# A gated mix of linear attention and a GLU: where the denominators of two token groups are summed, and where the T sums of p stand

## The chip, the cores and the metric

The kernel runs on one core of a Trainium2 chip. The metric is the device time of one execution in microseconds (us), lower is better. Before the change the median of three runs is 732.84 us (732.48 to 736.08).

## The reference

For 2048 tokens of width 640, two blocks read the same x and are mixed by a gate per token:

```python
def _A_ref(x, wqkv, wo):                 # linear attention, H = 32 heads, Dh = 20
    q, k, v = ...                        # (x @ wqkv), split by head
    phi = lambda t: jnp.where(t > 0, t + 1, jnp.exp(t)) + 1e-6
    pq, pk = phi(q), phi(k)
    kv = jnp.einsum("bhsd,bhse->bhde", pk, v)
    z = jnp.einsum("bhsd->bhd", pk)
    num = jnp.einsum("bhqd,bhde->bhqe", pq, kv)
    den = jnp.einsum("bhqd,bhd->bhq", pq, z)[..., None] + 1e-6
    return (num / den) ... @ wo
def _B_ref(x, w_gate, w_up, w_down):     # F = 1536
    return (_sigmoid(x @ w_gate) * (x @ w_up)) @ w_down
g = _sigmoid((x * gate_w).sum(-1, keepdims=True))
return g * a + (1 - g) * b
```

The change concerns den, the denominator of each token and head: the sum over 20 features of phi(q) times z.

## The kernel before, in words

All is computed transposed: features on the 128 partitions, tokens along the row. The tokens lie in four groups g of TG = 512. Products are made as three fp32r matmuls each (high and low halves, `mm3`, lines 407 to 409), and most products of 2x2 blocks with seven in place of eight products (the steps s1 to s7 of `Block`, line 1324, and `down_pair`, line 1976), whose sums are made by DVE.

The program has these stages: k and its statistics (to about 145 us); q for groups 2 and 3, with kv (`q_phase(1)`); the GLU for groups 2 and 3 (`f_phase(1)`, twelve blocks f of 128 features of F); q for groups 0 and 1 (`q_phase(0)`, about 407 to 446 us of the profile); the GLU for groups 0 and 1 (`f_phase(0)`, to about 665 us); and the product of scaled phi(q) with the folded kv and wo, with the final mix. The call with `pr = 0` is the second pass over the weights: there the forms of the weights made in the first pass are loaded again from DRAM. Each block f needs three tiles: wg, wu and ws (`load_form`, line 1236), issued on SP after the steps s2, s6 and s7 that read the old ones (line 2274). Each odd f from 3 on also runs `down_pair` for the two blocks ahead of it, with a tile wf in three transfers (`load_wf`, line 1668), issued after s7.

phi(q) without its 1e-6, which is added when it is read, is called p here. `phi_q` (line 1380) makes one tile of p, 128 x 512, for a group g and a feature chunk u (five chunks, KC = 5): ACT makes the exponential and the relu, DVE joins them (line 1388), and a POOL transfer stores the tile to `p_dram`. The feature axis is ordered so that each partition belongs to a head.

The denominators are made by `queue_dens` (line 1432). For each (g, u) a tile of p is read back from `p_dram` into a tile named pden (one of the four buffers of the pool tag "t"), and DVE adds p times `zcol[:, u]` to `fac[:, g]` (five sums per group, line 1442). Then POOL stores the sum to `den_dram`; SP reads it back turned, so that the four parts of a head meet (`turn_in`, four transfers named fac<-den_dram and one of gates, gs); DVE makes gate / den (`factor`: two adds, a reciprocal, a product); POOL stores it to `fac_dram`; and SP reads it back spread over the partitions (`turn_out`, four transfers fac<-fac_dram). `dens` (line 2219) starts groups 2 and 3 at f = 2 and groups 0 and 1 at f = 3 of pr = 0.

`queue_tp` (line 1792) makes the T sums: it reads eight tiles of p of groups 2 and 3 (tile pt), scales them by fac, and stores four sums and differences of each column to `pt_dram`. It is queued at f = 4. `queue_m` (line 1724) reads the folded matrix m (tile mr, four transfers), splits it and stores it to `mp_dram`, five times over, and then makes its sums (`queue_msf`); the first is called after (f, s) = (3, 7), line 2620.

The order on the engines is made by a planner, the class `Order` (line 31), as the program is built. It holds estimated times of PE, ACT and DVE. Work that may wait stands in lists (streams with due times, items, lazy, chain, spare), and `fill` (line 116) takes an item out when its data are expected to be there and it would end within a set slack of PE. `need(key)` runs a list up to that key at once. The engines then run what was written, each in that order; SP and POOL issue their transfers in the order of the program.

Of the kernel before, what the change touches and what calls it, by code (L numbers as in the profile page):

```python
# [374 lines left out]
def gated_mix_kernel(ctx: ExitStack, tc: tile.TileContext, xt, xn, wk, wv, wo, wst_q, wst_f, out_t):  # L375
# [46 lines left out]
    def vec2(out, a, b, op, after=""):  # L422
        order.on_vec(width(out), after, 1.0, out, a, b)
        nc.vector.tensor_tensor(out, a, b, op=op)  # L424

    def vec3(out, a, scalar, b, op0, op1, after=""):
        order.on_vec(width(out), after, 1.0, out, a, b)
        nc.vector.scalar_tensor_tensor(out, a, scalar, b, op0=op0, op1=op1)

    def vec1(out, a, s0, s1=None, op0=OP.mult, op1=None, after=""):  # L430
        order.on_vec(width(out), after, 1.0, out, a)
        if op1 is None:
            nc.vector.tensor_scalar(out, a, s0, None, op0=op0)
        else:
            nc.vector.tensor_scalar(out, a, s0, s1, op0=op0, op1=op1)
# [10 lines left out]
    def add(out, a, b, after=""):  # L446
        vec2(out, a, b, OP.add, after)
# [773 lines left out]
    def tt(name, dt=F32, shape=(P, TG)):  # L1221
        return pw.tile(list(shape), dt, name=name, tag="t", bufs=4)
# [101 lines left out]
    class Block:  # L1324
# [51 lines left out]
        def s7(self):  # L1376
            prod(self.cc, [self.xb(2, 2 + j, 2 + j) for j in range(2)] + [self.xb(2, 4, 4)], False)
            add(self.c12, self.cc, self.c12, "p")

    def phi_q(g, u, src, after="p"):  # L1380

        e = tt("qe")
        act(e, src, AF.Exp, after)
        r = src if after == "v" else tt("qr")
        act(r, src, AF.Relu)

        def rest():
            vec3(e, e, 1.0, r, OP.min, OP.add)
            gp.dma_start(p_dram[:, u, g], e)
        order.need("phi")  # L1390
        order.follow(v_cost(TG), rest, "phi")

# [34 lines left out]
    def gates():  # L1427
        if not gate_sum:
            gate_sum.append(down_pool[1].tile([P, TG], F32, name="gs", tag="far"))
        return gate_sum[0]  # L1430

    def queue_dens(*gs2):

        st = {}

        def load(g, u):
            if u < KC:
                st[g, u] = tt("pden")
                sp.dma_start(st[g, u], p_dram[:, u, g])
                st["at", g, u] = lambda: order.when(st[g, u]) + 1.5  # L1440

        def one(g, u):
            td = fac[:, g]
            if u == 0:
                vec1(td, st[g, u], zcol[:, 0:1], zeps[:, 0:1], OP.mult, OP.add)
            else:
                vec3(td, st[g, u], zcol[:, u:u + 1], td, OP.mult, OP.add)
            load(g, u + 2)
            if u == KC - 1:
                gp.dma_start(den_dram[:, g], td)  # L1450
                st["at", g, u + 1] = lambda: order.when(den_dram[:, g])

        def turn_in(g):
            for j in range(4):
                js = slice(j * H, (j + 1) * H)
                sp.dma_start(fac[js, g].rearrange("h (d c) -> h d c", c=P),
                                  den_dram[:, g, j * P:(j + 1) * P].rearrange("(d h) c -> h d c", h=H))
            st[g, "gs"] = gates()[:, g * P:(g + 1) * P]
            sp.dma_start(st[g, "gs"], gate_rep[4 * g:4 * g + 4].rearrange("i h c -> (i h) c"))
            st["at", g, KC + 1] = lambda: max(order.when(fac[:, g]), order.when(st[g, "gs"])) + 2.5  # L1460

        def factor(g):
            td = fac[:, g]
            q = td[:, :P]
            add(td[:, :2 * P], td[:, :2 * P], td[:, 2 * P:])
            add(q, q, td[:, P:2 * P])
            order.on_vec(5 * P, "")
            nc.vector.reciprocal(q, q)
            vec2(q, q, st[g, "gs"], OP.mult)
            gp.dma_start(fac_dram[:, g], q)  # L1470
            st["at", g, KC + 2] = lambda: order.when(fac_dram[:, g])

        def turn_out(g):
            for d in range(4):
                sp.dma_start(fac[d * H:(d + 1) * H, g].rearrange("h (j c) -> h j c", c=P),
                                  fac_dram[:, g].rearrange("(j h) c -> h j c", h=H))
            FAC_AT[g] = lambda: order.when(fac[:, g]) + 2.5
        order.add(0, 0, lambda: [load(g, u) for u in range(2) for g in gs2], chain=True)
        for u in range(KC):
            for g in gs2:  # L1480
                order.add(0, v_cost(TG), lambda g=g, u=u: one(g, u), None, lambda g=g, u=u: st["at", g, u](), chain=True)
        for n, (v, fn) in enumerate(((0, turn_in), (2.0, factor), (0, turn_out))):
            for g in gs2:
                order.add(0, v, lambda g=g, fn=fn: fn(g), ("fac", g) if n == 2 else None,
                          lambda g=g, n=n: st.get(("at", g, KC + n), lambda: 1e9)(), first=True)

    sp.t = max(sp.t, gp.cell[0])
    load_w()
# [256 lines left out]
    FAC_AT = {}  # L1745

    def queue_msf(i):

# [43 lines left out]
    def queue_tp(j):  # L1792

        src = ((2, j), (2, 2 + j), (3, j), (3, 2 + j))
        raw = []

        def load():
            for g, u in src:
                raw.append(tt("pt"))
                sp.dma_start(raw[-1], p_dram[:, u, g])  # L1800

        def total(n):
            b11, b21, b12, b22 = raw
# [427 lines left out]
    def f_phase(pr, q, hooks={}):  # L2231
# [70 lines left out]
        for f in range(FC):  # L2302
            if f % 2:
                order.need(("h", f // 2 - 1, "B22"), False)
            down = iter(())
            if not pr and f == 4:
                for j in range(2):
                    queue_tp(j)
            if f in dens[pr]:
                queue_dens(*dens[pr][f])  # L2310
            if f % 2 and f > 1:
                if pr:
                    pass
                elif f == FC - 1:
                    for g in range(4):
                        order.need(("fac", g), False)
                    load_m(0)
                down = down_pair(pr, f // 2 - 1)
            for s in (3, 4, 5):
                step(f, s)  # L2320
                next(down, None)
                if s == 3 and f % 2 and f > 1:
                    queue_h(f // 2 - 1, "T4")
                    queue_h(f // 2 - 1, "T3")
                if pr and s == 4:
                    if f < 2 or f % 2:
                        queue_d(("f", 1, f))
                    if f % 2 and f < FC - 1:
                        queue_ds(f // 2)
                    if f == 1:  # L2330
                        queue_df(0)
            if f + 1 < FC:
                step(f + 1, 1)
            else:
                queue_t1(f // 2)
                step(f, 6)
            for _ in down:
                pass
            if f % 2:
                if f < FC - 1:  # L2340
                    queue_t1(f // 2)
                if pr:
                    if f == FC - 1:
                        load_last_s()
                    elif f > 1:
                        queue_df(f // 2)
                    if f < FC - 1:
                        queue_d(("f", 1, f + 1))
            if f + 1 < FC:
# [264 lines left out]
    def a_fifth():  # L2614
# [330 lines left out]
```

## Time and profile before

| | before |
|---|---|
| median of three runs | 732.84 us |
| the profiled execution: its own time | 734.26 us |
| its span in the profile | 732.6 us |
| PE busy | 721.8 us, 99% of the span |
| DVE busy | 588.2 us, 80% |
| ACT busy | 370.0 us, 51% |
| mean rate of the DMA | 263 GB/s |

A row of the timeline gives the start in us from the span's start, the duration, the engine, the line of the kernel, the operation, the tile written and the tiles read (buffer numbers left out), the number of instructions, and in brackets how long the engine was idle before it and what ended that. SPq and POOLq are the queues of transfers that SP and POOL issue: the duration is that of the issue, not of the transfer. Matmuls overlap, so a row's duration is longer than the step from one matmul to the next.

### The profile page before, as it was taken

How to read it: one execution, taken by the hardware profiler on the slowest of the kernel's cores; microseconds unless marked ns; L12 is line 12 of the kernel's file. 1: busy time of each engine (PE TensorE's matmuls, PEld its weight loads, DVE VectorE, ACT ScalarE, POOL GpSimd, SP SyncE). 2: the span in 40 equal slices, each digit the busy share in tenths (PEclk: the TensorE clock that was granted, in tenths of full speed). 3: DMA queues.
4: the chain of work that ended last, by engine and by line, in shares of the span. 5: the costliest groups of instructions: out<-in, count | busy, mean ns of one | idle time of the engine just before them, and what ended most of it. 6: DMA issues, size and time to landing. Idle time of an engine off the chain costs nothing.

```text
span 732.6 us, 10285 instructions
## 1 busy us (share of the span) xinstructions
PE 721.8 (99%) x3545; PEld 617.1 (84%) x3545; DVE 588.2 (80%) x1026; ACT 370.0 (51%) x682; POOL 111.4 (15%) x180
## 2 busy tenths in 40 slices
PE   9999999999999999999999999999799999999998
PEld 8999999988888888888888888888588878787876
DVE  6898878987787889888999954568668789799894
ACT  5884649357667644444455754353324242445450
POOL 0211111113212211211111132000000011011200
PEclk9999999999999999999999999999999999999999
DMA  7577689698787856657687899869979897979946
GB/s 258 157 219 187 179 219 256 146 347 279 273 322 264 317 204 230 232 222 265 247 310 269 243 329 370 339 201 284 355 227 363 253 353 274 374 283 329 193 117 210
DMA packets 83034, 192.30 MB, mean 263 GB/s; under 512 B 12666, under 2 KB 40586, under 8 KB 79270
## 3 DMA queue, kind: packets, MB, share of 16 engines
q1 hardware_dynamic: 62598, 120.41, 49.8%
q0 software_dynamic: 20240, 71.06, 29.1%
q8 instruction: 28, 0.46, 0.3%
q14 instruction: 24, 0.20, 0.1%
q10 hardware_dynamic: 144, 0.16, 0.1%
HBM read 114.12 MB, written 73.56 MB: 256 GB/s over the span
## 4 chain that ended last, share of the span: by engine, by line
PE 85%; DMA 9%; DVE 3%; SPq 1%; ACT 1%; issue 1%; ACTq 0%; DVEq 0%
PE ch L407 9%; PE ch L408 9%; PE ch L409 9%; PE cc L407 8%; PE cc L408 8%; PE cc L409 8%; PE dd L407 6%; PE dd L408 6%; PE dd L409 6%; PE rot L408 5%; PE rot L407 5%; PE rot L409 5%; DMA wu<-wf 2%; DMA wf<-wd 2%; DMA mr<-m_dram 2%; DMA ws<-wf 1%
## 5 line engine op out<-in xcount | busy, mean ns | idle before, releaser
L420 ACT ACTIVATE c<-ch 128x512 f32<-128x512 f32 x54 | 32.2, 597 | 89.1 <-PE ch L409 84.6
L424 DVE TENSOR_TENSOR hf<-c,hf 128x512 fp32r<-128x512 f32 x80 | 54.5, 686 | 22.1 <-ACT hf L420 21.7
L420 ACT ACTIVATE hf<-c 128x512 fp32r<-128x512 f32 x80 | 49.0, 624 | 30.6 <-DVE c L424 30.5
L424 DVE TENSOR_TENSOR c<-cc,c 128x512 f32<-128x512 f32 x42 | 28.9, 689 | 33.8 <-ACT c L420 17.5
L407 PE MATMUL ch<-xth,ws 128*128 128x512 f32 x112 | 43.9, 392 | 2.2 <-DMA ws<-wf 2.2
L409 PE MATMUL ch<-xth,ws 128*128 128x512 f32 x112 | 43.6, 390 | 0.0
L408 PE MATMUL ch<-xtl,ws 128*128 128x512 f32 x112 | 43.6, 389 | 0.0
L424 DVE TENSOR_TENSOR tb<-rot,tb 128x512 f32<-128x512 f32 (+1 forms) x58 | 37.5, 674 | 3.6 <-PE rot L409 3.6
L424 DVE TENSOR_TENSOR c<-c,c 128x512 f32<-128x512 f32 x52 | 35.7, 687 | 1.8 <-ACT c L420 1.1
L407 PE MATMUL dd<-xrh,wg 128*128 128x512 f32 x90 | 35.2, 391 | 0.0
L409 PE MATMUL dd<-xrh,wg 128*128 128x512 f32 x90 | 35.0, 389 | 0.0
L408 PE MATMUL dd<-xrl,wg 128*128 128x512 f32 x90 | 35.0, 389 | 0.0
L420 ACT ACTIVATE c<-dd 128x512 f32<-128x512 f32 x22 | 13.1, 597 | 43.3 <-PE dd L409 43.2
L407 PE MATMUL cc<-xbh,ws 128*128 128x512 f32 x84 | 32.7, 389 | 0.0
L409 PE MATMUL cc<-xbh,ws 128*128 128x512 f32 x84 | 32.7, 389 | 0.0
L408 PE MATMUL cc<-xbl,ws 128*128 128x512 f32 x84 | 32.7, 389 | 0.0
L420 ACT ACTIVATE dd<-ch 128x512 f32<-128x512 f32 x22 | 12.8, 582 | 34.8 <-PE ch L409 34.8
L424 DVE TENSOR_TENSOR tb<-dd,tb 128x512 f32<-128x512 f32 x36 | 24.7, 685 | 5.7 <-PE dd L409 5.7
L407 PEld LDWEIGHTS ch<-xth,ws 128*128 128x128 f32 x112 | 21.0, 188 | 7.1 <-DMA ws<-wf 3.0
L424 DVE TENSOR_TENSOR wst<-wst 128x256 f32<-128x256 f32 (+1 forms) x65 | 24.6, 395 | 1.4
L424 DVE TENSOR_TENSOR tb<-cc,tb 128x512 f32<-128x512 f32 x36 | 24.5, 685 | 1.3 <-PE cc L409 1.3
L409 PEld LDWEIGHTS ch<-xth,ws 128*128 128x128 f32 x112 | 21.0, 188 | 4.7 <-DVE ws L424 0.2
(697 smaller groups left out, 2380.7 us busy)
## 6 DMA issues: line engine op xcount, KB each, us to landing
wf<-ws POOLq DMA_DIRECT2D x12, 1152.0 KB, 7.6
ws<-wf SPq DMA_DIRECT2D x11, 1152.0 KB, 7.9
wst<-wst_f SPq DMA_DIRECT2D x12, 640.0 KB, 5.1
wf<-wg POOLq DMA_DIRECT2D x12, 640.0 KB, 6.9
wd<-wd POOLq DMA_DIRECT2D x12, 640.0 KB, 8.0
wg<-wf SPq DMA_DIRECT2D x12, 640.0 KB, 6.9
wf<-wd SPq DMA_DIRECT2D x10, 640.0 KB, 9.5
xnst<-xn SPq DMA_DIRECT2D x16, 320.0 KB, 4.7
```

The source lines that it names most:

```text
L407: nc.tensor.matmul(out, l_hi, r_hi, start=first, stop=False, skip_group_check=True)
L408: nc.tensor.matmul(out, l_hi, r_lo, start=False, stop=False, skip_group_check=True)
L409: nc.tensor.matmul(out, l_lo, r_hi, start=False, stop=last, skip_group_check=True)
L420: nc.scalar.activation(out, src, fn, **kw)
L424: nc.vector.tensor_tensor(out, a, b, op=op)
```

## The change

- `phi_q`: for groups 0 and 1 the tile of p is multiplied by zcol and added to the denominator as soon as it is made (`den_term`), into a tile `den` of the pool's tag hf0 (four buffers), in place of `fac`. A new tile of p asks first that the denominator of the last but one be done (`order.need(("den", n - 2))`).
- The sum of a group ends with its store to `den_dram`. `queue_factor`, the old `turn_in`, `factor` and `turn_out` for one group, is called for groups 2 and 3 when their sum ends, and for groups 0 and 1 at f = 5.
- `queue_dens` is left for groups 2 and 3 alone, and starts at f = 3.
- The T sums wait for the factors of groups 2 and 3 alone.
- `queue_m` starts after (f, s) = (2, 7).

```diff
     def phi_q(g, u, src, after="p"):
 
+        n = phis.pop() + 1
+        phis.append(n)
+        order.need(("den", n - 2))
         e = tt("qe")
...
             gp.dma_start(p_dram[:, u, g], e)
+            if g < 2:
+                order.add(0, v_cost(TG), lambda: den_term(g, u, e), ("den", n), chain=True)
...
+    def den_term(g, u, src):
+
+        if g < 2 and not den_sum:
+            den_sum.append(down_pool[0].tile([P, 2, TG], F32, name="den", tag="hf0", bufs=4))
+        td = den_sum[0][:, g] if g < 2 else fac[:, g]
+        if g in DEN:
+            vec3(td, src, zcol[:, u:u + 1], td, OP.mult, OP.add)
+        else:
+            vec1(td, src, zcol[:, u:u + 1], zeps[:, 0:1], OP.mult, OP.add)
+        DEN[g] = DEN.get(g, 0) + 1
+        if DEN[g] == KC:
+            gp.dma_start(den_dram[:, g], td)
+            if g > 1:
+                queue_factor(g)
...
-                  [FAC_AT.get(g, lambda: 1e9)() for g in range(4)]) + 1, chain=True)
+                  [FAC_AT.get(g, lambda: 1e9)() for g in (2, 3)]) + 1, chain=True)
...
-    dens = ({2: (2, 3), 3: (0, 1)}, {})
+    dens = ({3: (2, 3)}, {})
...
+            if not pr and f == 5:
+                for g in range(2):
+                    queue_factor(g)
...
-        (3, 7): [queue_m],
+        (2, 7): [queue_m],
```

`queue_factor(g)` holds the three old steps for one group, and `order.add`s them as urgent items. The order of PE's instructions is the same before and after.

On SP, from the last pden load ahead of the wu of f = 5 to the transfers behind its wf (of before; the numbers tell the forms in DRAM apart):

```order
L364 DMA pden<-p_dram 128x512 x11
L364 DMA wu<-wf_2909 128x768
L364 DMA fac<-den_dram 32x4x128 x4
L364 DMA gs<-gate_rep 128x128
L364 DMA pden<-p_dram 128x512 x2
L364 DMA wg<-wf_3012 128x1280
L364 DMA fac<-den_dram 32x4x128 x4
L364 DMA gs<-gate_rep 128x128
L364 DMA pden<-p_dram 128x512
L364 DMA ws<-wf_2984 128x2304
L364 DMA mr<-m_dram 32x640 x4
L364 DMA wf<-wd_2832 128x2x640 x2
```

The same place on SP now:

```order
L364 DMA pden<-p_dram 128x512 x4
L364 DMA mr<-m_dram 32x640 x4
L364 DMA pden<-p_dram 128x512
L364 DMA wu<-wf_2909 128x768
L364 DMA wg<-wf_3012 128x1280
L364 DMA ws<-wf_2984 128x2304
L364 DMA wf<-wd_2832 128x2x640 x2
L364 DMA wf<-wd_2832 128x2x1024
L364 DMA mr<-m_dram 32x640 x4
L364 DMA fac<-den_dram 32x4x128 x4
L364 DMA gs<-gate_rep 128x128
```

The pden, fac, gs and mr transfers between the four weight transfers have moved ahead of them or behind them. Two blocks on, at f = 7, SP now has:

```order
L364 DMA mr<-m_dram 32x640 x4
L364 DMA fac<-fac_dram 32x4x128 x4
L364 DMA wu<-wf_3214 128x768
L364 DMA wg<-wf_3376 128x1280
L364 DMA ws<-wf_3289 128x2304
L364 DMA wf<-wd_3145 128x2x640 x2
```

Before, eight transfers fac<-fac_dram stood further ahead, and the fac<-den_dram and mr transfers stood between wu and wg.

On DVE, in the q blocks of groups 0 and 1 (qe is a new tile of p, xtl and c are forms and evictions that the matmuls use):

```order
L424 TENSOR_TENSOR xtl<-fac,xth 128x2x256 x2
L435 TENSOR_SCALAR den<-qe,zcol,zeps 128x512
L428 SCALAR_TENSOR_TENSOR qe<-qe,qr 128x512
L424 TENSOR_TENSOR xtl<-fac,xth 128x2x256
L424 TENSOR_TENSOR fac<-fac 128x512
L424 TENSOR_TENSOR xtl<-fac,xth 128x2x256
L435 TENSOR_SCALAR den<-qe,zcol,zeps 128x512
L424 TENSOR_TENSOR c_4350<-dd_4343,c_4350 128x512
L428 SCALAR_TENSOR_TENSOR qe<-qe,c_4251 128x512
L428 SCALAR_TENSOR_TENSOR den<-qe,zcol,den 128x512
```

Before, there are no den rows there, and the products tb<-tb,ds (the scaling by 1-g) begin one tile of p sooner; now a den row follows the qe rows, and those products come later.

More of the change, by code (lines that the diff above doesn't have):

```diff
@@ L1378, in s7 @@
             add(self.c12, self.cc, self.c12, "p")
+    phis = [0]
     def phi_q(g, u, src, after="p"):
+        n = phis.pop() + 1
+        phis.append(n)
+        order.need(("den", n - 2))
         e = tt("qe")
@@ L1430, in gates, with queue_factor, turn_in, factor @@
         return gate_sum[0]
+    DEN, FAC_AT = {}, {}
+    den_sum = []
+    def den_term(g, u, src):
[11 more added lines that the diff above has]
+                queue_factor(g)
+    def queue_factor(g):
+        td = fac[:, g]
+        at = [lambda: order.when(den_dram[:, g])]
+        gs = []
+        def turn_in():
+            for j in range(4):
+                js = slice(j * H, (j + 1) * H)
+                sp.dma_start(fac[js, g].rearrange("h (d c) -> h d c", c=P),
+                             den_dram[:, g, j * P:(j + 1) * P].rearrange("(d h) c -> h d c", h=H))
+            gs.append(gates()[:, g * P:(g + 1) * P])
+            sp.dma_start(gs[0], gate_rep[4 * g:4 * g + 4].rearrange("i h c -> (i h) c"))
+            at.append(lambda: max(order.when(td), order.when(gs[0])) + 2.5)
+        def factor():
+            q = td[:, :P]
+            add(td[:, :2 * P], td[:, :2 * P], td[:, 2 * P:])
+            add(q, q, td[:, P:2 * P])
+            order.on_vec(5 * P, "")
+            nc.vector.reciprocal(q, q)
+            vec2(q, q, gs[0], OP.mult)
+            gp.dma_start(fac_dram[:, g], q)
+            at.append(lambda: order.when(fac_dram[:, g]))
+        def turn_out():
+            for d in range(4):
+                sp.dma_start(fac[d * H:(d + 1) * H, g].rearrange("h (j c) -> h j c", c=P),
+                             fac_dram[:, g].rearrange("(j h) c -> h j c", h=H))
+            FAC_AT[g] = lambda: order.when(td) + 2.5
+        for n, (v, fn) in enumerate(((0, turn_in), (2.0, factor), (0, turn_out))):
+            order.add(0, v, fn, ("fac", g) if n == 2 else None, lambda n=n: at[n]() if len(at) > n else 1e9, first=True)
     def queue_dens(*gs2):
@@ L1439, in load @@
                 sp.dma_start(st[g, u], p_dram[:, u, g])
-                st["at", g, u] = lambda: order.when(st[g, u]) + 1.5
         def one(g, u):
[L1443 to L1447, printed above, removed]
-            load(g, u + 2)
[L1449 to L1477, printed above, removed]
+            den_term(g, u, st[g, u])
+            load(g, u + 2)
         order.add(0, 0, lambda: [load(g, u) for u in range(2) for g in gs2], chain=True)
@@ L1480, in queue_dens @@
             for g in gs2:
[L1481 to L1485, printed above, removed]
+                order.add(0, v_cost(TG), lambda g=g, u=u: one(g, u), "den", lambda g=g, u=u: order.when(st[g, u]) + 1.5, chain=True)
     sp.t = max(sp.t, gp.cell[0])
@@ L1744, in gated_mix_kernel @@
     pt_dram = dram.tile([P, 4, 2, TG], F32, name="pt_dram")
-    FAC_AT = {}
     def queue_msf(i):
```

## The prediction

> **What bounds the kernel now.** I began with the busy times and the list of what the matmul engine (PE) waited for.
>
> ```profile
> PE 721.8 (99%) x3545; PEld 617.1 (84%) x3545; DVE 588.2 (80%) x1026; ACT 370.0 (51%) x682; POOL 111.4 (15%) x180
> ```
>
> ```profile
> PE dd L407 <- DMA wf<-wd: 2.9, 3, 1.5
> PE ch L407 <- DMA ws<-wf: 2.2, 2, 1.8
> PE ch L408 <- DVE pq L424: 1.0, 1, 1.0
> PE ch L2700 <- ACT pq L420: 0.2, 1, 0.2
> ```
>
> PE is busy for 99% of the span. The instruction order shows the same matmuls in the same order before and after, so the change can only remove or add PE idle time. Of the waits listed, 5.1 us (2.9 and 2.2) end with the landing of a weight tile: ws (the sums of the gate and up weights) and wf (the forms of the down weights). I then looked for their place in the timeline of PE (start, duration, instruction, idle time before it).
>
> ```profile
> 513.46 0.39 PE L409 MATMUL cc<-xbh,ws 128*128 128x512 f32 x1
> 515.63 0.50 PE L407 MATMUL ch<-xth,ws 128*128 128x512 f32 x1 [1.79 <-DMA ws<-wf]
> 518.54 0.50 PE L407 MATMUL dd<-hf,wf 128*128 128x512 f32 x1 [1.26 <-DMA wf<-wd]
> 522.36 0.47 PE L407 MATMUL dd<-hf,wf 128*128 128x512 f32 x1 [1.46 <-DMA wf<-wd]
> ```
>
> Three stalls lie within 9 us, at block f = 5 of the second pass over the weights (pr = 0). The idle marks add to 4.51 us, but an idle mark is too small: PE starts a 128x512 matmul every 0.23 us while one is shown as 0.39 us long. So I counted matmuls in the stretches (first PE busy and its count, last the granted clock, the DMA share and GB/s).
>
> ```profile
> 420.00:512.00 92.00, 92.00 (x408) 76.13 (x407) 53.97 (x85) 41.99 (x73) 12.44 (x23) 1.00 0.87 305
> 512.00:560.00 48.00, 43.49 (x190) 35.02 (x189) 33.44 (x57) 15.77 (x29) 4.31 (x8) 1.00 0.90 309
> 560.00:600.00 40.00, 39.85 (x176) 32.48 (x175) 32.68 (x53) 15.31 (x27) 4.34 (x8) 1.00 0.90 301
> 600.00:640.00 40.00, 39.63 (x174) 32.09 (x173) 32.35 (x54) 12.82 (x23) 4.32 (x8) 1.00 0.90 333
> ```
>
> Undisturbed, a matmul takes 92.00/408 = 0.2255 us. At that pace 190 need 42.8 us of the 48, so the three stalls cost 5.2 us. The next two stretches lack 0.3 and 0.8 us by the same count. The clock is 1.00 in all four rows, so no part of this is a slower PE.
>
> Why were the tiles late? SP issues its transfers in program order, and these are its rows around that place and the same loads one block earlier.
>
> ```profile
> 473.08 0.32 SPq L364 DMA_DIRECT2D wu<-wf  x1
> 475.12 0.32 SPq L364 DMA_DIRECT2D wg<-wf  x1
> 477.16 0.32 SPq L364 DMA_DIRECT2D ws<-wf  x1
> ...
> 497.67 0.44 SPq L364 DMA_DIRECT2D wu<-wf  x1
> 499.15 1.74 SPq L364 DMA_DIRECT2D fac<-den_dram  x4
> ...
> 501.46 0.85 SPq L364 DMA_DIRECT2D pden<-p_dram  x2
> 503.05 0.32 SPq L364 DMA_DIRECT2D wg<-wf  x1
> 503.46 1.81 SPq L364 DMA_DIRECT2D fac<-den_dram  x4
> ...
> 506.32 0.38 SPq L364 DMA_DIRECT2D ws<-wf  x1
> 509.66 1.72 SPq L364 DMA_DIRECT2D mr<-m_dram  x4
> 511.42 1.84 SPq L364 DMA_DIRECT2D wf<-wd  x3
> ```
>
> A weight load may go out when PE has read the old tile. From wu to wu that is 24.59 us, so wg was due at 499.71 and ws at 501.75. They went at 503.05 and 506.32, 3.3 and 4.6 us late, with fac, gs and pden transfers of the denominators in between; wf, which could follow ws at once, went at 511.42 behind mr. ws was wanted at 513.69 (513.46 plus a matmul) and came 1.94 us later.
>
> **The change part by part.** *The queue of SP at f = 3 to 5.* By the order, wu, wg, ws and wf now stand one behind another, with the ten remaining pden loads ahead and the mr, fac and gs transfers behind. If the pden are through by 498, ws goes out at about 501.8 and wf at 502.2. Each keeps its own time of before: ws took from 506.32 to 515.63, at most 9.3 us, and would land at 511.1 against 513.69. The last part of wf took from 511.42 to 522.36, at most 10.9, and would land at 513.1, before wf is read at all. All 5.2 us go. What is late next has 2.6 us of room.
>
> *The pden loads and their sums.* Twenty loads of 256 KB become ten. The ten sums over p of groups 0 and 1 do not go away: they move to the q blocks, from about 414 to 446 us, and read the fresh tile. Here are the prices of one, its loads' landing, and that stretch (DVE is the third pair).
>
> ```profile
> L428 DVE SCALAR_TENSOR_TENSOR fac<-pden,zcol,fac x16: 740/743/749, 481.2 to 535.0; 128x512 f32<-128x512 f32 x16
> L435 DVE TENSOR_SCALAR fac<-pden,zcol,zeps x4: 540/540/543, 480.3 to 498.8; 128x512 f32<-128x512 f32 x4
> DMA to landing us min/median/max: 2.6/4.5/11.8
> ```
>
> ```profile
> 414.00:446.00 32.00, 32.00 (x149) 26.71 (x148) 20.73 (x33) 18.81 (x32) 13.39 (x24) 1.00 0.88 317
> ```
>
> Eight at 0.743 and two at 0.540 are 7.0 us, and DVE is idle for 11.3 us of these 32, so they fit; PE does not wait there (32.00 of 32). I charge nothing. The cover is DVE's idle time between evictions; were it gone, they would cost at most their 7.0 us, and no gain is possible where PE has no wait. Behind them the ten products tb by 1-g and their stores end some us later; the first wf load waits for these stores, and its block is first used after the ws row at 477.16, some 30 us on: nothing. The den tile takes one turn of the four hf0 buffers, which come round again only in the f blocks: nothing. The two den stores move from 495 on to the q blocks, on a POOL queue that then carries p and tb: nothing, since PE waits for neither.
>
> *The factors of the four groups.* Their transfers in (fac, gs) move behind wf, and the transfers out stand as four single groups on SP. The first stands directly ahead of wu, wg, ws and wf for f = 7, and waits for the store of its factor. In DVE's order the first factor stands where the last pden sum stood. Rows: that sum, the first and last instruction of a factor, and how long its store took to land (median of three).
>
> ```profile
> 534.97 0.74 DVE L428 SCALAR_TENSOR_TENSOR fac<-pden,zcol,fac 128x512 f32<-128x512 f32 x1
> ```
>
> ```profile
> 512.90 0.74 DVE L424 TENSOR_TENSOR fac<-fac 128x256 f32<-128x256 f32 x2
> ...
> 514.67 0.29 DVE L424 TENSOR_TENSOR fac<-fac,gs 128x128 f32<-128x128 f32 x1
> ```
>
> ```profile
> fac_dram<-fac POOLq DMA_DIRECT2D x3, 64.0 KB, 6.9
> ```
>
> Less the 5.2 us, the factor starts at 529.8 and ends 2.1 later, at 531.9; its store lands at 538.8. SP issues the four transfers out (1.8 us, as fac at 503.46) by 540.6 and reaches ws at 541.5 and wf at 541.9. For what follows: issue and landing of the same loads before, and where PE used them.
>
> ```profile
> 545.91 0.38 SPq L364 DMA_DIRECT2D ws<-wf  x1
> 546.34 1.80 SPq L364 DMA_DIRECT2D wf<-wd  x1
> ```
>
> ```profile
> ws<-wf SPq DMA_DIRECT2D x1, 1152.0 KB, 7.9
> ...
> wf<-wd SPq DMA_DIRECT2D x1, 640.0 KB, 9.1
> ```
>
> ```profile
> 555.80 0.39 PE L407 MATMUL ch<-xth,ws 128*128 128x512 f32 x1
> ...
> 557.16 0.39 PE L407 MATMUL dd<-hf,wf 128*128 128x512 f32 x1
> ```
>
> PE will want ws at 550.6 and wf at 552.0 (5.2 less). Issue plus 7.9 and 9.1 gives 549.4 and 551.0: in time, by 1.2 and 1.0 us. This is the tightest place that I see, so I charge 0.4 us, between nothing and the 3 us of the first rival.
>
> Here a page of the Trainium skill gives another price. "DMA: Bandwidth & Descriptors", Anatomy of one DMA, puts a transfer issued from GpSimd at about 2.0 us plus its bytes at 436 GB/s, an estimate of 2.2 us for this 64 KB store. The trace shows 6.9, so the row decides; by the page the store lands 4.7 us sooner, SP would not be held, and the charge of 0.4 would be nothing.
>
> *The T sums and the m loads.* These are the stretches that lack 0.3 and 0.8 us. The mr and mv transfers stood between the wg and the ws load of f = 9 and of f = 11; now they stand ahead of those weights' loads or earlier, and the m chain starts a block sooner. I take both as gone: 1.1 us, between 0 and 1.1. The sums still read p from DRAM, and their multiplications keep their number, so their other cost is nothing.
>
> *The end.* The scaling of the last pl tiles moves ahead, so the wait of 0.2 us for pq goes. The wait of 1.0 us for DVE's pq stays, because DVE's order ahead of it is unchanged.
>
> The sum: 5.2 + 1.1 + 0.2 - 0.4 = 6.1 us. The profiled execution took 734.26 us and would take 728.2. The median of the three runs is 732.84, 1.4 us lower; with the same stalls in them the forecast is 732.84 - 6.1 = 726.7 us.
>
> **The rivals.** *The stall moves to f = 7 (730).* SP is held by the first transfer out for longer than I count. For it speaks that the loads there have only 1.0 us of room, and that POOL once stood long before a factor's store:
>
> ```profile
> 515.25 0.54 POOL L364 DMA_DIRECT2D fac_dram<-fac  x1 [18.92 <-DMA mr<-m_dram]
> ```
>
> Against it: in that order most of the 18.92 us is POOL having nothing to do. If the store is 4.3 us later, PE waits 3.3 us: 726.7 + 3.3 = 730.0.
>
> *The rate of the DMA is the limit (728).* POOL's stores share the 16 engines with the weights. mp stores of 640 KB now begin at f = 3, and with two den stores of 256 KB 1152 KB could fall on ws and wf at f = 5: 3.7 us at the 309 GB/s of the row from 512 to 560. The room was 2.6 us, so 1.1 remain, with a restart 1.3: 728.0. Against it: half of the pden bytes are gone. The Trainium skill, "DMA: Bandwidth & Descriptors", Queues, rings and completion order, says that an engine takes packets in turn from the queues that have work; by that rule POOL's stores would indeed push the weights back here, as this rival has it. The runs before do not part that from SP's late issue.
>
> *DVE stands still for a pden load at f = 3 (729).* The loads begin behind ws of 477.16, not 15 us ahead of use.
>
> ```profile
> 488.00 0.69 DVE L424 TENSOR_TENSOR c<-cc,c 128x512 f32<-128x512 f32 x1 [3.04 <-ACT c L420]
> ```
>
> This idle time of 3.04 us ahead of an eviction covers a late landing; with the slowest landing of before, 11.8, from about 480.5 (ws, four mr and some pden issued), the data come at 492.3 and evictions slip by over 4 us, of which PE, which reuses the rot banks after three products (2.0 us), would lose some 2.3: 729.0. Against it: DVE waited for no pden load before.
>
> *SP's order of transfers out backfires (slower).* The same mechanism as the first rival, but the store's turn on POOL comes after an mp store whose mr load and split are late, and SP stands with all weights of f = 7 behind it. If the store waits as long as the row above shows, 18.9 us, PE loses 17.9: 744.6. It is slower than before once the wait exceeds 6.1 + 1.0 = 7.1 us.
>
> **How the numbers follow.** The forecast has 0.58, the first rival 0.20, the DMA rate 0.10, DVE's wait 0.08, the slower one 0.04. What this measurement can tell from no change is about 0.5%, 3.7 us, so faster means below 729.2: forecast, DMA rate and DVE's wait, 0.76; the first rival is "same", 0.20; slower 0.04. The low end of the range is the forecast without the 0.4 and with the 1.0 us wait at the end gone too, 725.3, rounded down to 725.0; the high end takes in the first rival with half a us more, 730.5. The forecast's own range is 725.3 to 728.
>
> **What would show it.** Right: no PE wait for ws or wf between 505 and 520; SP's wu, wg, ws and wf in a row near 502; about 213 matmuls in the 48 us from 512; DVE nearly full from 414 to 446 and PE still without a gap there. Wrong: a PE wait for wf or ws at 550 (first rival) or still at 514 (DMA rate), a DVE wait for pden near 486, or a PE wait for DVE from 420 to 450. If the weight stalls vanish and the time does not fall by 4 us or more, my reading that PE's gaps set the time is wrong.

## The result, and the profile after

After the change the median is 726.89 us (726.29 to 727.67, four runs), beside 733.17 us before in the same job: a ratio of 0.9907, interval 0.9879 to 0.9936. A later job gave 727.51 (six runs) beside 732.37 (23 runs): 0.9938, interval 0.9918 to 0.9959. So the change saves 4.9 to 6.3 us. The kernel before spreads from 729.48 to 735.99 in one job, the changed one from 726.83 to 727.94. With 23 runs against six this suggests, but does not show, that what went is a part of the time that also varied from run to run.

The profiled execution took 727.67 us (before 734.26). Busy times, and PE's waits by what ended them (total, times, longest), of after:

```profile
PE 719.6 (99%) x3545; PEld 616.7 (85%) x3545; DVE 587.2 (81%) x1026; ACT 369.4 (51%) x682; POOL 111.5 (15%) x180
```

```profile
PE ch L408 <- DVE pq L424: 0.9, 1, 0.9
PE rot L495 <- PEq L2958: 0.8, 1, 0.8
PE cc L407 <- DVE tb L424: 0.7, 1, 0.7
PE rot L407 <- DVE tb L424: 0.2, 1, 0.2
```

DVE is as busy as before (588.2), so no work was saved there. No wait for ws or wf is left; a wait for DVE's tb is new. The stretches of after, as in the prediction's table (PE first, then PEld, DVE, ACT, POOL, each with its count, then the clock, the DMA share and GB/s):

```profile
414.00:446.00 32.00, 32.00 (x148) 26.70 (x147) 24.70 (x39) 18.71 (x33) 12.32 (x22) 1.00 0.87 300
512.00:560.00 48.00, 48.00 (x213) 39.64 (x212) 35.06 (x59) 16.86 (x30) 3.23 (x6) 1.00 0.82 272
560.00:600.00 40.00, 39.10 (x172) 31.62 (x171) 30.43 (x51) 13.03 (x23) 3.78 (x7) 1.00 0.95 350
600.00:640.00 40.00, 40.00 (x178) 33.07 (x177) 33.88 (x57) 12.28 (x22) 3.24 (x6) 1.00 0.78 274
```

From 512 to 560 PE runs 213 matmuls in place of 190: 23 x 0.2255 = 5.2 us more work. From 600 to 640 it gains four, 0.9 us. But from 560 to 600 it runs 172 in place of 176, 0.9 us less. SP around f = 5, after:

```profile
496.93 0.34 SPq L364 DMA_DIRECT2D pden<-p_dram  x1
497.37 0.72 SPq L364 DMA_DIRECT2D wu<-wf  x1
499.02 0.32 SPq L364 DMA_DIRECT2D wg<-wf  x1
501.06 0.32 SPq L364 DMA_DIRECT2D ws<-wf  x1
501.44 2.18 SPq L364 DMA_DIRECT2D wf<-wd  x3
```

wu, wg, ws and wf stand one behind another; ws goes out 5.3 us earlier than before, wf 10.0 us.

The new stall at 563, as PE, DVE and SP show it:

```profile
562.95 0.50 PE L407 MATMUL cc<-hf,wf 128*128 128x512 f32 x1 [0.67 <-DVE tb L424]
```

```profile
561.40 0.43 DVE L424 TENSOR_TENSOR mv<-mv 128x256 f32<-128x256 f32 x1 [2.48 <-DMA mv<-m_dram]
```

```profile
548.50 8.43 SPq L364 DMA_DIRECT2D mr<-m_dram  x4
556.97 2.53 SPq L364 DMA_DIRECT2D mv<-m_dram  x4
```

SP's own waits from 540 to 562 name the reason:

```profile
SPq L364 <- DMA wf<-wd: 6.0, 3, 3.1
SPq L364 <- DMA ws<-wf: 1.1, 1, 1.1
```

DVE stood 2.48 us for mv, with the evictions tb behind it, because SP took 8.43 us to issue four mr of 80 KB ahead of it, most of it waiting for the landing of wf, though mr has no use for wf. By the steps between matmuls PE lost 1.4 us here (0.9 at 563, 0.5 at 564).

### The profile page after: what moved, and what is told of

It is laid out like the page before. It is cut to its first block, busy times and chain, and to the rows that moved or that the text cites. A ratio compares the mean times of both kernels' runs of the same rounds, so it can differ in the third digit from the quotient of the medians.

```text
span 726.0 us, 10253 instructions
## 1 busy us (share of the span) xinstructions
PE 719.6 (99%) x3545; PEld 616.7 (85%) x3545; DVE 587.2 (81%) x1026; ACT 369.4 (51%) x682; POOL 111.5 (15%) x180
## 4 chain that ended last, share of the span: by engine, by line
PE 94%; DMA 2%; DVE 2%; SPq 1%; issue 0%
PE ch L408 10%; PE ch L407 10%; PE ch L409 10%; PE cc L407 8%; PE cc L409 8%; PE cc L408 8%; PE dd L407 7%; PE dd L408 7%; PE dd L409 7%; PE rot L407 5%; PE rot L408 5%; PE rot L409 5%; DMA wf<-wd 2%; SPq L364 1%; DVE hf L428 1%; PE rot L1577 1%
## 5 line engine op out<-in xcount | busy, mean ns | idle before, releaser
L424 DVE TENSOR_TENSOR hf<-c,hf 128x512 fp32r<-128x512 f32 x80 | 54.4, 686 | 19.3 <-ACT hf L420 18.9
L409 PEld LDWEIGHTS ch<-xth,ws 128*128 128x128 f32 x112 | 21.0, 188 | 4.7 <-DVE ws L424 0.3
L408 PEld LDWEIGHTS ch<-xtl,ws 128*128 128x128 f32 x112 | 21.0, 188 | 4.3
```

Of the source, the lines that this page charges most:

```text
L408: nc.tensor.matmul(out, l_hi, r_lo, start=False, stop=False, skip_group_check=True)
L409: nc.tensor.matmul(out, l_lo, r_hi, start=False, stop=last, skip_group_check=True)
```

## The experiments

My theory: PE stood at f = 5 because SP issued ws and wf late, behind other transfers; the bytes matter less, and the moved sums cost nothing. The rivals: bytes; the moved sums; the turn of the m chain.

**SP held with hardly a byte.** Changed kernel, with three 64 KB transfers ahead of ws, each waiting for the last:

```diff
+                    if (f, i) == (3, 2):
+                        nc.sync.dma_start(hold_dram[0], p_dram[:, 0, 0, :P])
+                        nc.sync.dma_start(hold_dram[1], hold_dram[0])
+                        nc.sync.dma_start(hold_dram[2], hold_dram[1])
                     load_form(("f", 0, f + 2), i)
```

> The kernel after, with three copies of 64 KB in a chain (each reads what the one before wrote; nothing else reads them) on SP between wg and ws of f = 5: SP is held for two landings, 4 to 6 us, with hardly a byte more. Late issue on SP: ws goes out at 505 to 507 as before the change, and PE waits for ws and wf at f = 5 for 2 to 5 us in all; the time is 729 to 732. Rate of the DMA: the bytes are those of the kernel after, so no wait over 1 us and 727 to 728.

Measured: 732.69 us, 1.0003 of before (0.9988 to 1.0019). SP, then PE, of this run:

```profile
508.53 0.53 SPq L364 DMA_DIRECT2D ws<-wf  x1
509.11 2.28 SPq L364 DMA_DIRECT2D wf<-wd  x3
```

```profile
514.00 0.50 PE L407 MATMUL ch<-xth,ws 128*128 128x512 f32 x1 [0.16 <-DMA ws<-wf]
516.56 0.51 PE L407 MATMUL dd<-hf,wf 128*128 128x512 f32 x1 [0.90 <-DMA wf<-wd]
520.55 0.47 PE L407 MATMUL dd<-hf,wf 128*128 128x512 f32 x1 [1.65 <-DMA wf<-wd]
```

ws goes out 8.94 us behind wg, in place of 2.04 in the changed kernel: 2.2 us later than before the change, and later than I expected. This brings the stalls for wf back and, with one of 0.80 at 555, takes the whole gain away (one of 1.1 at 569 is the changed kernel's stall of 0.67 at 563, grown). A late issue is enough for wf. It is not for ws: PE waits 0.16 us for it here and 1.79 before the change, though it goes out later here, because it lands 5.4 us after its issue in place of some 9.3. Before the change wg was still under way when ws went out (it landed at 509.58), here it was not (504.99). So what was under way ahead of ws seems to have had a part in that old wait; no run shows how much.

**More bytes, issued elsewhere.** Changed kernel, with seven transfers of 256 KB, DRAM to DRAM, on POOL's queue at the end of f = 3:

```diff
                     load_form(("f", 0, f + 2), i)
+                    if (f, i) == (3, 1):
+                        for u in range(7):
+                            nc.gpsimd.dma_start(spare_dram[:, u], p_dram[:, u % KC, u // KC])
```

> The kernel after, with seven transfers of 256 KB from DRAM to DRAM (copies of p that nothing reads) issued by POOL after step 6 of f = 3, near 497: 1.8 MB, as many bytes as SP moved between wu and wf before. Late issue on SP: ws and wf had 2 us and more of room, so at most 1.5 us of PE wait for ws or wf at f = 5 and a time within 2 us of the kernel after (727 to 729). Rate of the DMA: 1.8 MB at 309 GB/s is 5.8 us, which pushes ws and wf back past their use; 3 us or more of PE wait at f = 5 and 730 or more.

Measured: 731.12 us, 0.9981 (0.9968 to 0.9995): some 4 us lost by the medians, 2.5 by the spans of the two profiles (728.5 and 726.0). From 505 to 520 the row of before, of after, then that of this run:

```profile
505.00:520.00 15.00, 11.96 (x52) 9.26 (x51) 11.02 (x19) 4.97 (x9) 0.54 (x1) 1.00 1.00 303
```

```profile
505.00:520.00 15.00, 15.00 (x68) 12.38 (x67) 9.00 (x14) 7.48 (x14) 0.55 (x1) 1.00 0.87 303
```

```profile
505.00:520.00 15.00, 14.68 (x63) 11.20 (x62) 7.92 (x14) 6.74 (x13) 0.55 (x1) 1.00 1.03 398
```

PE runs five matmuls fewer than after the change (1.1 us), and stands 0.77 us for wf at 554. Each side was half right: the wait at f = 5 is within my 1.5 us, the time within the rival's 730 or more. Bytes do count: ws landed 12.4 us after its issue in place of 8.2, the last part of wf 19.3 in place of 15.8. But a full share does not decide alone. Of the runs below, two have a share of 1.03 and 1.04 from 505 to 520 and no stall there (the fresh-tile denominators alone, and only the loads gone); with SP held as above it was 0.82, with fourteen small transfers 0.76, and the stalls were back.

**The weights on another queue.** The kernel before, with ws and wf of f = 5 issued by POOL, so that no pden, fac or mr stands ahead of them:

```diff
+                    sp.engine = nc.gpsimd if (f, i) == (3, 2) else nc.sync
                     load_form(("f", 0, f + 2), i)
+                    sp.engine = nc.sync
```

and the same around `load_wf` at f = 3.

> The kernel before, all its pden reads kept; only the ws load of f = 5 and the three wf loads behind f = 3 are issued by POOL in place of SP, so that they need not stand behind fac, gs, pden and mr. Late issue on SP (my theory): ws and wf go out near 502, the three PE stalls of 512 to 523 (5.2 us) shrink to 1 us or less, the time falls by 4 to 5 us to about 728.5. Rate of the DMA (rival: the bytes of pden are what counts): the same bytes move, at least 3.5 of the 5.2 us stay, and the time is 731.5 or more.

Measured: 736.09 us, 1.0052 (1.0033 to 1.0072), slower: my expectation failed. PE's waits for ws and wf at f = 5 were gone, but these stood in their place (PE, ACT, DVE, SP, and the stretch):

```profile
522.15 0.79 PE L407 MATMUL dd<-hf,wf 128*128 128x512 f32 x1 [4.97 <-ACT dd L420]
```

```profile
520.88 0.74 ACT L420 ACTIVATE mt<-mr 128x640 fp32r<-128x640 f32 x1 [4.53 <-DMA mr<-m_dram]
```

```profile
520.24 0.75 DVE L428 SCALAR_TENSOR_TENSOR fac<-pden,zcol,fac 128x512 f32<-128x512 f32 x1 [7.99 <-DMA pden<-p_dram]
```

```profile
509.30 7.26 SPq L364 DMA_DIRECT2D mr<-m_dram  x4
```

```profile
505.00:512.00 7.00, 7.00 (x32) 5.82 (x31) 6.08 (x10) 2.45 (x5) 0.01 (x1) 1.00 1.01 402
```

ACT's eviction dd stands in order behind the split of mr, which landed late: from 505 to 520 SP waited 3.1 us for wg to land, 5.3 for fac and 2.2 for pden before it could issue more (the part on four small transfers below says why). So moving the weights forward without taking anything out only makes the other transfers late; the share is 1.01. The change takes ten loads out as well.

**Only the loads gone.** The kernel before, but the ten loads of p for groups 0 and 1 left out, DVE doing ten instructions of that size on resident data in about the old place (so these denominators hold no p; the first of each five is a fill):

```diff
             if u < KC:
+                if g < 2:
+                    st["at", g, u] = st.get(("at", g, u - 1), lambda: 0)
+                    return
...
+                    vec3(td, td, zcol[:, u:u + 1], td, OP.mult, OP.add)
```

> The kernel before, in which the denominators of groups 0 and 1 are made of no p at all: their ten loads of p are left out, and DVE does ten instructions of the same size on resident data at the old place (so these denominators are wrong). All else is as before, with the m chain at its old place, so it takes ten transfers of 256 KB off SP at f = 3 to 5 and leaves DVE's work where it was. Theory (what SP issues ahead of ws and wf of f = 5): fac and gs of both pairs still stand ahead of wg, but ws follows wg at once; the waits for ws go and at most 1 us for wf stays, 727.5 to 729 us, the old 1.1 us from 560 to 640 apart. Rival (moving the sums off DVE at f = 3 to 5 is what helped): no more than 1 us is gained, 731 us.

Measured: 729.60 us, 0.9965 (0.9948 to 0.9981). All stalls of f = 5 are gone; what is left is elsewhere (PE's waits):

```profile
PE ch L408 <- DVE pq L424: 0.9, 1, 0.9
...
PE dd L407 <- ACT dd L420: 0.6, 1, 0.6
PE ch L407 <- DMA ws<-wf: 0.6, 1, 0.6
PE ch L2709 <- ACT pq L420: 0.2, 1, 0.2
```

The wait for ws is at 587, that for ACT at 629. DVE still did its ten instructions at f = 3 to 5 (from 495 to 511; the sums before from 497 to 536), so the rival that their move helped falls. The time is 0.6 us above the 729 that I expected, with such waits from 560 to 640 left out of that sum.

**Fresh-tile denominators alone.** The changed kernel with the old starts of the sums of groups 2 and 3 and of the m chain, and T sums that wait for all four factors:

```diff
-                  [FAC_AT.get(g, lambda: 1e9)() for g in (2, 3)]) + 1, chain=True)
+                  [FAC_AT.get(g, lambda: 1e9)() for g in range(4)]) + 1, chain=True)
-    dens = ({3: (2, 3)}, {})
+    dens = ({2: (2, 3)}, {})
-        (2, 7): [queue_m],
+        (3, 7): [queue_m],
```

> The denominators of groups 0 and 1 from the fresh tiles alone: the sums of groups 2 and 3 start at f = 2 as before the change, the m chain starts after (3, 7) as before, and the T sums wait for all four factors. Theory (the place of transfers on SP ahead of ws and wf of f = 5 decides): the ten pden loads are through early, so ws goes out in time, but an mr still stands ahead of wf, which keeps a wait of 0 to 2 us, and the 1.1 us from 560 to 640 stay: 728 to 731 us. Rival (the bytes decide): half the pden bytes are gone, so all stalls at f = 5 go: 727 to 728 us. Third (the turn of the m chain is what helps, as the slow run with the later m chain suggests): 733 us or more.

Measured: 727.80 us (727.17 to 728.20), 0.9935 (0.9911 to 0.9958). No stall is left at f = 5; PE waits for ACT's dd at 591 (0.69) and for pq at 690 (1.17). This lies inside both intervals of the whole change: the other turn of the sums adds nothing that these runs can tell. It is the result that the rival named (no stall, 727 to 728); I had kept a wait for wf behind mr, but wf, issued at 505.22, came in time. The run takes out bytes and transfers at once, so its time does not part the two. From 505 to 520 its engines move more than before the change (303 GB/s), and PE has no gap:

```profile
505.00:520.00 15.00, 15.00 (x68) 12.38 (x67) 12.79 (x22) 7.72 (x14) 1.60 (x3) 1.00 1.03 387
```

**The two turns by themselves.** First the changed kernel with the m chain back at (3, 7), then the kernel before with the m chain at (2, 7):

```diff
-        (2, 7): [queue_m],
+        (3, 7): [queue_m],
```

> The kernel after with one part undone: the m chain starts after step 7 of f = 3 again, not of f = 2. The planner then puts mr, fac and gs between ws and wf of f = 5, and mr between wg and ws of later blocks. Late issue on SP: wf of f = 5 is late again, PE waits 1 to 4 us at f = 5 to 9, and the time is 728 to 731. If the denominators alone made the gain: within 1 us of the kernel after.

> The kernel before with one line of the change: the m chain starts after (2, 7) in place of (3, 7). All twenty loads of p for the denominators stay. On SP one mr, fac and gs then stand ahead of or behind ws of f = 5, and wf follows fac. Theory (what SP issues between wg and ws, and between ws and wf, decides, and small transfers count there): ws still goes out late behind pden, fac and mr, so 2 to 4 of the 5.2 us at f = 5 remain: 729 to 732 us. Rival (the turn of the m chain alone brings the gain, and the denominators only came with it): 727 to 728 us.

Measured: 736.81 us, 1.0062 (1.0041 to 1.0083), and 734.36 us, 1.0028 (1.0011 to 1.0045): both slower than before, and slower than I expected (728 to 731, and 729 to 732). That the turn of the m chain alone makes the gain falls with the second. SP of the first at f = 5, and PE's first wait there:

```profile
500.94 0.32 SPq L364 DMA_DIRECT2D ws<-wf  x1
501.30 1.97 SPq L364 DMA_DIRECT2D mr<-m_dram  x4
503.38 6.90 SPq L364 DMA_DIRECT2D fac<-den_dram  x4
510.33 0.43 SPq L364 DMA_DIRECT2D gs<-gate_rep  x1
510.80 2.74 SPq L364 DMA_DIRECT2D wf<-wd  x3
```

```profile
516.37 0.50 PE L407 MATMUL dd<-hf,wf 128*128 128x512 f32 x1 [1.86 <-DMA wf<-wd]
```

Here ws goes out early, but mr, fac and gs stand ahead of wf, and four fac of 64 KB take 6.90 us to issue. The steps between matmuls show 5.1 us lost from 514 to 522, 1.6 at 594 and 3.4 from 658 to 664, the last behind DVE's tb; why DVE was late there was not followed. In the second the stalls at f = 5 were 3.2 us, as expected (2 to 4), but a further 3.0 us came at 554 to 559, where I expected none (idle 0.74 for ws, 0.69 and 0.78 for wf). So in these runs the later start of the sums of groups 2 and 3 did well only with the earlier m chain, and the earlier m chain only with the ten loads gone.

**Why four small transfers hold SP.** In the order of each engine SP's transfers take eight semaphores in turn, and each waits for the one before it on its semaphore, eight places ahead (before, then the changed kernel with fourteen transfers of 2 KB added, seven ahead of ws and seven ahead of wf):

```
179 L364 DMA wg<-wf_3012 128x1280 [waits DMAHW6_49,PE_49]
187 L364 DMA mr<-m_dram 32x640 [waits DMAHW6_49,DMASW2_49,DMASW1_49]

176 L364 DMA wg<-wf_3013 128x1280 [waits DMAHW6_49,PE_49]
184 L364 DMA ws<-wf_2985 128x2304 [waits DMAHW6_49,PE_49]
192 L364 DMA wf<-wd_2833 128x2x640 [waits DMAHW6_49]
```

```diff
+                    for u in range(7 if (f, i) == (3, 2) else 0):
+                        nc.sync.dma_start(tiny_dram[u:u + 1], p_dram[u:u + 1, u % KC, 0])
                     load_form(("f", 0, f + 2), i)
+                    for u in range(7, 14 if (f, i) == (3, 2) else 7):
+                        nc.sync.dma_start(tiny_dram[u:u + 1], p_dram[u:u + 1, u % KC, 0])
```

> The changed kernel with fourteen more transfers of 2 KB (DRAM to DRAM, read by nobody) on SP at the end of f = 3: seven ahead of ws and seven between ws and wf. By the program each transfer of SP waits for a semaphore that the transfer eight places ahead of it sets as it lands. Theory (a count of eight transfers under way holds the queue, whatever they carry): ws cannot go out before wg has landed (about 504.5), nor wf before ws has landed (510 to 511), so wf is as late as before the change: 3 to 5 us of waits for ws and wf at f = 5, 730 to 733 us. Rival (only the time of issuing counts, 0.35 us each, 28 KB being nothing): ws at about 504 and wf at about 507, at most 0.6 us of waits, 727 to 728 us.

Measured: 732.19 us, 0.9994 (0.9977 to 1.0010). SP and PE of this run:

```profile
499.82 0.32 SPq L364 DMA_DIRECT2D wg<-wf  x1
500.19 4.33 SPq L2297 DMA_DIRECT2D tiny_dram<-p_dram  x7
505.88 0.33 SPq L364 DMA_DIRECT2D ws<-wf  x1
506.25 5.59 SPq L2300 DMA_DIRECT2D tiny_dram<-p_dram  x7
513.25 2.84 SPq L364 DMA_DIRECT2D wf<-wd  x3
```

```profile
518.42 0.57 PE L407 MATMUL dd<-hf,wf 128*128 128x512 f32 x1 [2.99 <-DMA wf<-wd]
```

wg landed 6.0 us after 499.82 and ws 7.4 us after 505.88: ws and wf go out at just these moments, 505.8 and 513.2. So the count does hold the queue, and 28 KB cost the whole gain. But the holding is only a part of the delay: SP's waits from 499 to 514 are 1.3 us for wg and 1.4 for ws, and the issues themselves took 0.62 and 0.80 us each on average, where the rival reckoned 0.35. This run does not tell how much the count costs alone. That it is not the bytes is plain from the engines, which were less busy than after the change (0.87):

```profile
505.00:520.00 15.00, 12.01 (x51) 9.59 (x50) 7.27 (x12) 4.01 (x8) 0.55 (x1) 0.96 0.76 262
```

Of the kernel before, SP's waits from 506 to 513 show the same at its mr:

```profile
SPq L364 <- DMA wg<-wf: 2.9, 1, 2.9
```

**The price of the sums in the q blocks.** The changed kernel with each of the ten terms added twice (so these denominators hold each term about twice):

```diff
+        if g < 2:
+            nc.vector.scalar_tensor_tensor(td, src, zcol[:, u:u + 1], td, op0=OP.mult, op1=OP.add)
```

> The changed kernel, in which each of the ten terms of the denominators of groups 0 and 1 is added a second time, so that the denominators are wrong (each holds its terms about twice). It prices the ten sums in the q blocks. Ten more instructions of 0.54 to 0.74 us are 7 us of DVE from 414 to 446, where the changed kernel's DVE was busy for 24.70 of 32 us. Theory (the sums lie in idle time of DVE between evictions and cost PE nothing): with 7.3 us idle they just fit, PE loses at most 2 us, 727 to 729 us. Rival (each DVE instruction pushes the evictions behind it, so the first ten also cost something that another gain hid): PE waits for DVE all through the q blocks, 4 to 7 us, 731 to 734 us.

Measured: 728.86 us, 0.9949 (0.9932 to 0.9966). The stretch:

```profile
414.00:446.00 32.00, 31.52 (x144) 25.93 (x143) 29.83 (x47) 18.42 (x32) 11.37 (x21) 1.00 0.84 290
```

DVE is busy for 29.83 of the 32 us and PE has one stall there, 0.75 us by the steps between matmuls (after: none). The first ten cost PE nothing that its row shows; the median is 1.4 to 2.0 us above the changed kernel's two, taken in other jobs, so the next ten cost little.

**A version that beats both.** The changed kernel, with the m sums taken into DVE's order 4 us later (for the stall at 563), first alone, then with the halves of pq of group 0 made ahead of those of group 1 at the end:

```diff
-                      lambda: max(order.when(r) for r in raw) + 2, spare=True)
+                      lambda: max(order.when(r) for r in raw) + 6, spare=True)
...
+            queue_pq(0)
             queue_pq(1)
-            queue_pq(0)
...
     order.fill()
+    for u in range(KC):
+        order.need(("pq", 1, u))
```

The last two lines take the halves of group 1 right behind `a_unit`, ahead of the last two blocks.

> The changed kernel, with the sums of the folded matrix (which read mr and mv back) taken 4 us later into DVE's order. In the changed kernel DVE stood 2.5 us for mv at about 560 and PE then lost 1.4 us at 563 to 564. Theory: DVE's order was written too early for a transfer that SP issued late, so with the larger margin DVE meets its data, the PE wait for tb at 563 goes, and nothing else moves: 726.9 - 1.4 = 725.5 us. Rival: the late mv only moves DVE's stall to another place, or the later sums push another transfer back: 726.9 or more, with a wait of PE for DVE somewhere from 560 to 640.

> A version meant to be faster than the changed kernel: the larger margin of the m sums, as tried alone before, and at the end of the program the high and low halves of pq of group 0 are made ahead of those of group 1, since PE reads group 0 first. Theory (PE's wait for DVE's pq at about 690, 0.9 to 1.2 us with its restart, is DVE making group 1's halves first): the wait goes, 725 to 726 us, 1.5 to 2.4 us below the changed kernel in the same job. Rival (the halves of group 1 or pt are then late, and the wait comes back behind a_unit): no faster than the margin alone, 726 to 727 us.

> The changed kernel itself, run beside the three others of this job, so that they have it to be compared with on the same chip: 726 to 728 us, 0.991 of the kernel before.

Measured: the margin alone 726.38 us (725.90 to 726.92), 0.9916 (0.9892 to 0.9940), in a job without the changed kernel; both 726.08 us (725.62 to 726.33), 0.9920 (0.9901 to 0.9938), beside 727.51 (726.83 to 727.94) for the changed kernel in the same job. With both, PE's waits are one row, at the program's start:

```profile
PE rot L495 <- PEq L2960: 0.8, 1, 0.8
```

Both stalls went, 2.6 us by the steps between matmuls; the medians differ by 1.4, just short of the 1.5 to 2.4 that I expected, and the margin alone was 0.9 us short of its 725.5. The two profiles account for the rest: wg for f = 4, whose place was not touched, went out at 475.31 in this run and at 474.56 in the changed kernel's, and 0.3 us went between matmuls at 700. By the ratios, 0.9916 and 0.9920, the second step adds nothing to the first that these runs can tell, though its wait is gone. From 410 us on no wait of PE is listed any more.

## Why the prediction was right, point by point

The forecast was 726.7 us; the two jobs gave 726.89 and 727.51.

- **The queue of SP at f = 3 to 5, 5.2 us.** Right: 213 matmuls from 512 to 560, as forecast, and the hold of SP brings the stalls back. The issue came as forecast: pden through by 497.3 (I had 498), ws at 501.06 (501.8), wf at 501.44 (502.2). Wrong was the room. The last part of wf (1024 KB) landed 15.8 us after its issue, at about 518.7, and PE read it at 519.23 at the earliest: perhaps only 0.5 us of room, not 2.6. I had taken 10.9 us from the stall at 522.36, but before the change this part landed 11.8 us after its issue, at about 524.4, so that stall was for the part ahead of it; and I had let each load keep its old landing time, though ws, of 1152 KB, now stood right ahead.
- **What held SP.** I had read the time of issuing and PE's release of the old tile. The count of eight transfers under way was not in my sum; it does not hold the weights of f = 5 in the new order, but it is behind 0.7 us of wg's lateness before (a wait for wu), 2.9 us of mr's and of wf's behind it, behind the 6.90 us of fac with the late m chain, and behind the new stall: the four mr at 548.50 stand eight places behind ws and wf of f = 7.
- **The ten sums in the q blocks, nothing.** Right: PE has no gap, and a second ten cost PE 0.75 us. My sign that DVE would be nearly full did not come: it is busy for 24.70 of 32 us, 4.0 more than before and not 7.0, because four of the ten products tb now come after 446.
- **The transfers out at f = 7, 0.4 us.** Not charged by the chip: no wait there. The first factor's store went out at 530.68 (I had 531.9 for the factor's end) and landed in 2.4 us, at 533.08, where I took 6.9. SP came to the transfers out only at 535.89, behind fac, gs and mr, so the store did not hold it, and wf was issued at 539.57 in place of 541.9. The estimate of 2.2 us from the Trainium skill, "DMA: Bandwidth & Descriptors", Anatomy of one DMA, was nearer for this store; for the third, issued at 539.24 just ahead of a 640 KB mp store, the trace has 7.3 us.
- **The T sums and the m loads, 1.1 us.** This step failed: the two stretches lacked 0.3 and 0.8 us before and lack 1.2 and 0 now. The old stalls did go, but the m chain made one of 1.4 us at 563, of a kind that I had not named, a DVE wait for mv.
- **The end, 0.2 us.** Right: ACT's pq no longer appears, DVE's stays with 0.9.
- **The sum.** 5.2 - 0.1 + 0.2 makes 5.3 us by counted matmuls. The profiled executions differ by 6.6: some 0.6 of it lies ahead of all that moved PE (wg for f = 4 went out at 474.54 in place of 475.12), and with its restart the wait of 0.2 was 0.6 by the steps between matmuls. That leaves some 0.3, little more than one matmul of the count. So 726.7 was met in part by luck: the counted matmuls give 0.8 us less than my 6.1 (the 1.1 did not come, nor the charge of 0.4), and the 0.6 ahead of all that moved, which the change did not make, filled most of the gap. The 732.84 that I started from is a median of three; the jobs with 23 and 30 runs have 732.07 to 732.37, and the job with more runs of both kernels a gain of 4.9.
- **The rivals.** DVE's wait for a pden load came, 1.9 us, and PE lost nothing by it. The rate of the DMA did not make PE wait after the change: from 503 to 516 the share is 1.01 after the change too, and PE has no gap. 1.8 MB more did cost PE 1.1 us there. SP's transfers out did not hold the weights of f = 7. The slower end was not far, though by another road: with the old m chain the same edit is slower than before.

## What to carry to other kernels

When a weight load is late, list what stands ahead of it on its queue and count transfers as well as bytes: where a program lets only a fixed number be under way, as this one does, a handful of small ones behind a large one holds the next weight until the large one has landed. Taking transfers out was worth more here than moving them: moving the weights ahead, or moving one chain alone, only made something else late. And check the room of the last part of a group of loads by the whole group's bytes, not by its own old landing time.

## What the runs showed of the hardware

After some stalls PE's granted clock fell to half. In the run with fourteen small transfers (the stall at 518, then 2.8 us, then full again):

```profile
515.00:518.40 3.40, 0.43 (x2) 0.01 (x1) 0.69 (x1) 1.12 (x2) 0.00 (x0) 1.00 0.93 322
518.40:519.20 0.80, 0.78 (x2) 0.63 (x3) 0.00 (x0) 0.00 (x0) 0.00 (x0) 0.69 1.14 407
519.20:522.00 2.80, 2.80 (x8) 2.23 (x7) 0.00 (x0) 0.58 (x1) 0.00 (x0) 0.50 1.03 385
522.00:525.00 3.00, 3.00 (x14) 2.43 (x14) 1.94 (x4) 2.63 (x6) 0.00 (x0) 0.98 0.70 138
```

In the third row a matmul follows the last by 0.43 us in place of 0.2255: a wait of 2.99 us cost PE 3.15 and then 1.7 us more. The same followed 4.97 us with the weights on POOL and 1.86 us with the late m chain (0.50 from 517.3 to 519.7), but not 2.70 us at 661 in that run, nor the three stalls before the change. The Trainium skill, "TensorE: Matmul & The Clock Gate", Part 1, has the clock halved after an idle window of about 3.4 us that runs free of the program. That the length of the wait does not decide alone fits a window that runs free. But 2.99 and 1.86 us are shorter than the window, so no whole window was idle there; where the measurement differs it decides, and what set the clock back in these two runs stays open.
